# Forgetting attention with a SwiGLU block: q and k loaded by casting transfers, their factor moved behind the transpose

## The chip, the cores and the metric

The kernel runs on one core of one Trainium2 chip. A core has five engines with a queue of instructions each: PE (TensorE, matmuls and transposes; its weight loads are listed as PEld), DVE (VectorE), ACT (ScalarE), POOL (GpSimd) and SP (SyncE, which here only issues transfers). Besides these, 16 DMA engines move data between HBM and SBUF, 128 partitions wide; PE writes into PSUM, eight banks of 512 f32 values in each partition, and the other engines copy out of it. A transfer that SP or ACT issues goes through the hardware queues (q1 and q10 in the profile), one that POOL issues through the software queue (q0). In this kernel only the software queue's transfers change the type on the way, f32 in HBM to bfloat16 in SBUF.

The metric is the device time of one launch in microseconds (us). Of the kernel before there are three timed runs and one profiled execution.

## The reference

```python
# q, k, v: (8, 8, 576, 64) f32;  f: (8, 8, 576);  x: (4608, 512)
scores = np.matmul(q, k.transpose(0, 1, 3, 2)) / np.sqrt(64)      # factor 1/8
cum    = np.cumsum(np.log(np.clip(f, 0.0001, 1.0)), axis=-1)
decay  = cum[:, :, :, None] - cum[:, :, None, :]
scores = np.where(causal, -1e9, scores + decay)                   # row >= column
attn   = exp(scores - max) / (sum + 1e-9)
x      = np.matmul(attn, v).transpose(0, 2, 1, 3).reshape(4608, 512)
g, val = x @ w_gate, x @ w_val                                    # 512 -> 1536
out    = (g / (1 + np.exp(-g)) * val) @ w_out                     # 1536 -> 512
```

All matmuls of the kernel are in bfloat16 with f32 sums.

## The kernel before

**Tiling.** Two heads of a batch make a pair; there are 32 pairs p (four to a batch), each with 576 rows of q in nine blocks of 64. Block i of both heads lies on the 128 partitions at once (64 rows of either head), so a score tile is 128 by up to 512. A pair is worked in two groups, g = 0 with blocks 0 to 3 and g = 1 with blocks 4 to 8. For that, q is kept turned, 64 head values on partitions, with one head in the upper and one in the lower half of buffer `qz` and zeros in the other places; k is kept turned in `kt`.

**A pair's way.** SP loads k and q as f32 (line 453, buffers `kf` and `qf`); a row of a partition holds 6 consecutive rows of k (96 partitions) or 8 of q (72 partitions), for both heads. POOL copies them to bfloat16 (lines 481 and 483, buffers `qb` and `kb`), q times -1/8, and puts the two heads beside each other. PE transposes (line 207, `tx` in PSUM); ACT or DVE copies `tx` out to `kt` (one copy) or `qz` (two) at lines 509 and 511. PE forms the scores (line 201, `sp`); DVE adds the running sums of log f (`cb`), and for pairs from 16 on also a mask (`cm`), and takes the minimum of a row in the same instruction (line 652); ACT forms the exponential and its row sum (line 672, `e`); POOL scales each row by the reciprocal (line 708, `pk`). The probabilities are transposed into `pT`, for pairs 0 to 7 on PE with copies out (lines 737 to 743), for pairs from 8 on by a transfer that SP issues (line 721). PE multiplies with v (line 764), and the result is stored turned in `xT`, which holds a ring of 2048 tokens.

**The feed-forward part.** It goes over 12 tiles of tokens (256, 256, seven of 512, 256, 128, 128) as soon as their rows of `xT` are there: matmuls with `wg` and `wv` into `gv`, tanh on ACT (line 855), two products on DVE (lines 857 and 860), matmuls with `wo`, a copy out (lines 884 and 886), a transfer to HBM. The weights are loaded once, by POOL with a cast on the way (line 824 for `wg` and `wv`, in pieces of 256, 256, 512 and 512 columns each; line 828 for `wo`).

**The first four pairs** (`NHALF`) have a way of their own: their k and q come in parts (rows 0 to 255 and 256 to 575, of two neighbouring pairs together for k and for the first part of q), loaded at line 534, copied to bfloat16 at lines 560 to 564 on POOL, ACT or DVE, transposed, and copied out at lines 589 and 591. Their running sums are picked out by a matmul with ones (line 425) and copied to `cb` (line 430).

**The order.** All operations are first collected with a cost on each engine that may do them, the buffers that they read and write, and a priority. A planner (lines 63 to 195) then picks the operation that can start first by these costs, the smaller priority at a tie, gives it an engine and a buffer, and so writes out one order for each engine. `SLACK` says how long a buffer may be kept for a more urgent user. `STARTUP` is the order of the first transfers, written out by hand (k0: second part of k of pair 0; p4: k and q of pair 4; c: running sums; v01: part 1 of v of batch 0; wv2: the piece of `wv` that begins with column 256, and so on). A weight transfer on POOL also waits for the loads five places before it in that list and for the POOL load two before it. `NUDGE` shifts the priorities of single units (q4: all that prepares k and q of pair 4; a5.1: pair 5, group 1; f2: tile 2 of the feed-forward part; o: its second half; v: v of a batch). Loads of later pairs wait for the row sums of the pair four before.

```python
engs = {"POOL": 850 if p < 8 else 800 if name == "k" else 1010}
...
bufs("qb", [P, ROWS["q"][1], 2, D], BF16, 2)
bufs("kb", [P, ROWS["k"][1], 2, D], BF16, 2)
```

Of the kernel before, what the change touches and what calls it, by code (L numbers as in the profile page):

```python
# [8 lines left out]
F32 = mybir.dt.float32  # L9
# [198 lines left out]


def mm(*cols):  # L210
    return sum(max(29, c / 2.4 + 2.5) for c in cols)
# [3 lines left out]
def kernel(  # L215
# [45 lines left out]
    JFROM = 8  # L261
    TWO = False
    NDIRECT = 0

# [20 lines left out]
    NUDGE = "a0.0:-6 a1.0:-12.5 a10.0:1 a10.1:1.5 a12.0:-0.5 a13.0:0.5 a13.1:-1 a15.0:-1 a15.1:1 a16.0:-3 a17.0:-2 a17.1:-1.5 a18.0:-0.5 a21.0:-1 a21.1:-1 a22.1:0.5 a25.1:-1 a26.1:-1.5 a27.0:-1.5 a27.1:1 a29.0:2 a30.1:-1 a31.0:0.5 a31.1:0.5 a4.0:2.5 a4.1:2.5 a5.0:-1.5 a5.1:-1 a6.0:0.5 a6.1:1 a7.1:-0.5 a8.0:-1 a9.1:-0.5 f0:4 f1:2 f11:-4 f3:-5 f4:-3.5 f5:-4 f6:-2 f7:1 f8:9.5 f9:0.5 o0:-1 o1:-991 o10:-12.5 o11:3.5 o4:1 o5:-7 o6:-4.5 o8:1 o9:9 q0:-8.5 q1:-12 q10:-1.5 q11:-3 q12:-1.5 q13:-3 q14:-4 q15:-2 q16:-6 q17:1.5 q18:-4 q19:-2 q2:-10 q21:0.5 q24:0.5 q26:2.5 q27:0.5 q29:-2 q3:-9.5 q30:-4 q4:-7 q5:-5 q6:-1 q8:-1 v1:-5.5 v2:-2 v3:3.5 v4:1.5 v5:5.5 v6:0.5 v7:-5"  # L285

# [154 lines left out]
    def half(key):  # L441
        return pl.buf(key).bitcast(BF16)


    def load_pair(p):
        b, hp = divmod(p, NPB)
        s = first[p]
        if p < NHALF:
            load_parts(p)
            return  # L450
        for name, src, pr in (("k", k, 0), ("q", q, .1)):
            pl.key((name + "f", p), name + "f")
            loads[name, p] = pl.op({"SP": 620} if p else {"ACT": 620}, lambda e, name=name, src=src: (nc.scalar if e == "ACT" else nc.sync).dma_start(
                out=pl.buf((name + "f", p))[0:ROWS[name][0], :, :],
                in_=src[b, 2 * hp:2 * hp + 2].rearrange("h (p r) d -> p h (r d)", r=ROWS[name][1])),
                (), [(name + "f", p)], (-99 + 3 * p if p < NPB else s - SOON) + pr, dma=1060, pk=68 if name == "k" else 86, after=[sums[p - BACK, 0 if p - BACK >= NPB else 1]] if p >= NPB else [])
        if p >= NSEL:
            pl.key(("cb", p), "cb", p)
            for h in range(2):
                loads["cb", p, h] = pl.op({"SP": 600}, lambda e, h=h: nc.sync.dma_start(  # L460
                    out=pl.buf(("cb", p))[64 * h:64 * h + 64, :],
                    in_=cum_dram[2 * p + h:2 * p + h + 1, :].to_broadcast((64, S))),
                    ["cum_dram"], [("cb", p), (("cb", p), 3)], -98.5 + 3 * p if p < NPB else s - SOON + .2, dma=570, pk=93, after=[sums[p - CBACK, 0 if p - CBACK >= NPB else 1]] if p >= NPB + 1 else [])

    def prepare(p):
# [4 lines left out]
        for name in ("k", "q"):  # L470
            fk, bk = (name + "f", p), (name + "b", p)
            KR, KC = ROWS[name]
            pl.key(bk, name + "b")

            def cast(e, name=name, fk=fk, bk=bk, KR=KR):
                src = pl.buf(fk)[0:KR, :, :].rearrange("p h (r d) -> p r h d", d=D)
                dst = pl.buf(bk)[0:KR, :, :, :]
                if e == "ACT":
                    nc.scalar.activation(dst, src, AF.Copy, scale=-scale if name == "q" else 1.0)
                elif name == "q":  # L480
                    eng[e].tensor_scalar(dst, src, -scale, 1.0, op0=ALU.mult, op1=ALU.mult)  # L481
                else:
                    eng[e].tensor_copy(dst, src)
            engs = {"POOL": 850 if p < 8 else 800 if name == "k" else 1010}
            if p < NPB:
                engs = {"POOL": 850, "ACT": 850, "DVE": 500} if name == "k" else {"POOL": 1050, "ACT": 1050, "DVE": 680}
            o = pl.op(engs, cast, [fk], [bk], s - 1 + (name == "q") * .1)
            o.bias = SPARE if p else {}
            tk = ("tt", name, p)
# [4 lines left out]
            def transpose(e, bk=bk, tk=tk, KR=KR, KC=KC):  # L494
                src = pl.buf(bk).rearrange("p r h d -> p r (h d)")
                for j in range(KC):
                    turned(nc, half(tk)[:, KR * j:KR * j + KR], src[0:KR, j, :], ident[0:KR, 0:KR])
            pl.op({"PE": KC * (KR / 2.4 + 2.5)}, transpose, [bk], [tk, ok], s - 1, lat=200)
            halves = [(0, P, None)] if name == "k" else [(0, 64, 0), (64, 128, 1)]
            for a, z, h in halves:  # L500
                def evac(e, a=a, z=z, h=h, tk=tk, ok=ok, KC=KC):
                    if h is None:
                        src = half(tk)[a:z, 0:S].rearrange("r (j p) -> r p j", j=KC)
                        dst = pl.buf(ok)[a:z, :].rearrange("r (p j) -> r p j", j=KC)
                    else:
                        src = half(tk)[a:z, 0:S].rearrange("r (j i p) -> r i j p", j=R, i=NB)
                        dst = pl.buf(ok)[a:z, :, h, :].rearrange("r i (j p) -> r i j p", j=R)
                    if e == "ACT":
                        nc.scalar.copy(dst, src)  # L509
                    else:  # L510
                        nc.vector.tensor_copy(dst, src)
                o = pl.op({"ACT": 600, "DVE": 680 if h is None else 390}, evac, [tk] + ([("z", "qz", p)] if h is not None and p < len(pl.pools["qz"]) else []), [ok, (ok, "done")], s - .9)
                o.bias = LATER if p >= 8 else {}
# [9 lines left out]
    def load_parts(p):  # L523
        b, hp = divmod(p, NPB)
        pl.key(("cb", p), "cb", p)
        for name, x, a, z, r, n in parts(p):
            fk = (name + "f", p, x)
            pl.key(fk, name + "f")
            m = (z - a) // r

            def load(e, u, fk=fk, src=(k if name == "k" else q), a=a, z=z, r=r, m=m):
                h0 = 2 * (hp + u)
                (nc.scalar if e == "ACT" else nc.sync).dma_start(  # L533
                    out=pl.buf(fk)[m * u:m * u + m, :, 0:r * D],
                    in_=src[b, h0:h0 + 2, a:z].rearrange("h (p r) d -> p h (r d)", r=r))
# [12 lines left out]
    def prepare_parts(p):  # L548
        for name, x, a, z, r, n in parts(p):
            fk, bk, tk = (name + "f", p, x), (name + "b", p, x), ("tt", name, p, x)  # L550
            m = (z - a) // r
            pr = min(at[p + u, x == "B"] for u in range(n)) - 1 + (name == "q") * .1
            pl.key(bk, name + "b")
            pl.key(tk, "tx", line="q")

            def cast(e, name=name, fk=fk, bk=bk, r=r, w=m * n):
                src = pl.buf(fk)[0:w, :, 0:r * D].rearrange("p h (r d) -> p r h d", d=D)
                dst = pl.buf(bk)[0:w, 0:r, :, :]
                if e == "ACT":
# [13 lines left out]
            def transpose(e, bk=bk, tk=tk, r=r, w=m * n):  # L573
                src = pl.buf(bk).rearrange("p r h d -> p r (h d)")
                for j in range(r):
                    turned(nc, half(tk)[:, w * j:w * j + w], src[0:w, j, :], ident[0:w, 0:w])
            pl.op({"PE": r * (m * n / 2.4 + 2.5)}, transpose, [bk], [tk] + (oks if x == "A" else []), pr, lat=200, holds=oks)
# [239 lines left out]
    def weights():  # L817
        def piece(engs, fn, reads, writes, *a, **kw):
            loads[writes[0]] = pl.op(engs, fn, reads, writes, *a, **kw)

        cuts = [0, 256, 512, 1024, 1536]
        for a, z in zip(cuts, cuts[1:]):
            for nm, wt, src in (("wg", wg, moe_w_gate), ("wv", wv, moe_w_val)):
                piece({"POOL": 600}, lambda e, wt=wt, src=src, a=a, z=z: nc.gpsimd.dma_start(
                    out=wt[:, :, a:z], in_=src[:, a:z].rearrange("(ko p) n -> p ko n", p=P)),
                    (), [(nm, n) for n in range(a // P, z // P)], 2 + a / 256, dma=5.1 * (z - a) + 880, pk=20 if z - a == 256 else 42)
        for c in range(0, KF, 4):
# [120 lines left out]
    def unit(o):  # L948
        w = o.writes[0] if isinstance(o.writes[0], tuple) else (o.writes[0],)
        n, *i = w[0] + w[1:] if isinstance(w[0], tuple) else w  # L950
        if n in ("kb", "qb", "kt", "qz", "cm", "kf", "qf", "cb") or n == "tt" and isinstance(i[0], str):
            return f"q{i[0] if n != 'tt' else i[1]}"
# [52 lines left out]
```

## Time and profile before

| | before |
|---|---|
| median of 3 runs | 414.56 us (410.96, 414.56, 416.29) |
| profiled execution | 415.21 us |
| its span in the trace | 413.4 us, granted clock of TensorE 1.00 |
| PE busy | 392.5 us, 95% |
| DVE busy | 333.2 us, 81% |
| ACT busy | 320.5 us, 78% |
| POOL busy | 271.1 us, 66% |
| read from and written to HBM | 46.65 MB, 9.58 MB |
| bytes moved by all transfers | 72.16 MB, mean 175 GB/s |

An engine is busy while it executes; issuing a transfer, waiting and branching are not counted. The span goes from the first to the last instruction in the trace. A group of the profile reads: line, engine, operation, written buffer, read buffer, shapes, how many; then busy us in all, mean ns of one, and after the next bar the idle us of the engine just ahead of these instructions with what ended most of it. The chain of waits follows the end of the span back through what each step waited for.

### The profile page before, as it was taken

What the parts mean: (1) busy time and instruction counts of PE and PEld (TensorE: products, weight loads), DVE (VectorE), ACT (ScalarE), POOL (GpSimd) and SP (SyncE); (2) the same over time, 40 slices, a digit from 0 to 9 for tenths busy, and PEclk for the clock granted to TensorE, in tenths of its full rate; (3) what the DMA queues carried; (4) which work ended last, traced back from release to release, by engine and by line L of the source; (5) the groups of instructions that cost most, each with busy time, mean ns of one, the idle gap of its engine ahead of it and who ended that gap; (6) DMA issues with size and microseconds to landing.
All of it is one profiled execution on the core that took longest, in us unless ns stands there. A gap on an engine that the chain in (4) does not pass through costs nothing.

```text
span 413.4 us, 15350 instructions
## 1 busy us (share of the span) xinstructions
PE 392.5 (95%) x5848; PEld 269.3 (65%) x5848; DVE 333.2 (81%) x1270; ACT 320.5 (78%) x904; POOL 271.1 (66%) x475
## 2 busy tenths in 40 slices
PE   3988988889999999999999999999999999999996
PEld 2667878777666765567776666665566555568775
DVE  4799987798999789999998999899989952775232
ACT  5799988799999998979998897998899653332221
POOL 7679966699996887799789798878777340000000
PEclk9999999999999999999999999999999999999999
DMA  7999979879799999999999999978996744000211
GB/s 192 190 216 226 216 126 247 163 189 210 184 230 191 229 196 233 241 203 230 224 196 223 234 210 225 239 215 182 201 223 114 149 93 126 2 2 28 79 53 52
DMA packets 144026, 72.16 MB, mean 175 GB/s; under 512 B 117904, under 2 KB 131728, under 8 KB 143952
## 3 DMA queue, kind: packets, MB, share of 16 engines
q1 hardware_dynamic: 137856, 66.21, 74.4%
q0 software_dynamic: 5808, 4.72, 7.9%
q8 instruction: 45, 0.74, 0.8%
q14 instruction: 29, 0.24, 0.2%
q10 hardware_dynamic: 288, 0.26, 0.2%
HBM read 46.65 MB, written 9.58 MB: 136 GB/s over the span
## 4 chain that ended last, share of the span: by engine, by line
PE 81%; DMA 6%; DVE 5%; ACT 3%; issue 2%; POOL 1%; SPq 1%; POOLq 0%; ACTq 0%
PE gv L201 63%; PE sp L201 9%; PE tx L764 4%; PE tx L207 3%; DMA wg<-in_moe_w_gate_dram 3%; DVE t L652 3%; DMA kf<-in_k_dram 2%; PE gv L207 2%; DMA vf<-in_v_dram 1%; ACT eo L672 1%; ACT e L672 1%; SPq L533 1%; POOL vt L811 0%; DVE th L857 0%; ACT kt L509 0%
## 5 line engine op out<-in xcount | busy, mean ns | idle before, releaser
L652 DVE CUSTOM_DVE_ANT_0 t<-sp,cb 128x320 f32<-128x320 f32 (+7 forms) x272 | 121.7, 463 | 9.7 <-PE sp L201 5.1
L708 POOL TENSOR_SCALAR pk<-e,lr 128x512 bf16<-128x512 f32 (+3 forms) x189 | 101.5, 541 | 41.9 <-DVE lr L690 19.7
L201 PE MATMUL gv<-xT,wg 128*64 128x512 bf16 (+2 forms) x1152 | 112.7, 326 | 2.5 <-issue 1.4
L201 PE MATMUL gv<-xT,wv 128*64 128x512 bf16 (+2 forms) x1152 | 112.4, 326 | 0.1
L201 PE MATMUL gv<-wo,hh 128*64 128x512 bf16 (+1 forms) x888 | 106.5, 373 | 0.0
L857 DVE SCALAR_TENSOR_TENSOR th<-th,gv 128x512 f32<-128x512 f32 x108 | 73.9, 684 | 31.3 <-ACT th L855 30.5
L672 ACT ACTIVATE e<-t,tm 128x448 f32<-128x448 f32 (+4 forms) x160 | 88.9, 557 | 5.1 <-DVE tm L652 4.7
L855 ACT ACTIVATE th<-gv 128x512 f32<-128x512 f32 x108 | 64.3, 595 | 35.8 <-PE gv L201 35.2
L201 PE MATMUL sp<-kt,qz 128*64 128x512 bf16 (+7 forms) x640 | 77.9, 294 | 5.3 <-DVE tm L652 3.4
L708 POOL TENSOR_SCALAR pk<-eo,lr 128x256 bf16<-128x256 f32 (+3 forms) x128 | 70.4, 550 | 12.3 <-DVE lr L690 9.0
L201 PEld LDWEIGHTS <-wg 128*64 128x64 bf16 x1152 | 58.8, 110 | 30.0 <-issue 1.6
L201 PEld LDWEIGHTS <-wv 128*64 128x64 bf16 x1152 | 59.8, 110 | 27.4 <-issue 0.4
L860 DVE TENSOR_TENSOR hh<-th,gv 128x512 bf16<-128x512 f32 x108 | 73.7, 684 | 4.8 <-PE gv L201 1.8
L672 ACT ACTIVATE eo<-t,tm 128x256 f32<-128x256 f32 (+3 forms) x128 | 71.3, 558 | 4.3 <-DVE tm L652 3.1
L201 PEld LDWEIGHTS <-hh 128*64 128x64 bf16 x888 | 50.7, 110 | 31.3
L201 PEld LDWEIGHTS <-qz 128*64 128x64 bf16 x640 | 41.7, 113 | 23.0 <-issue 5.9
L884 ACT ACTIVATE ot<-gv 128x512 f32<-128x512 f32 (+1 forms) x34 | 19.9, 584 | 26.2 <-PE gv L201 26.0
L652 DVE DVE_READ_ACCUMULATOR2_ANT tm<- 128x1 f32 x432 | 35.7, 83 | 0.0
L652 DVE CUSTOM_DVE_ANT_0 t<-sp,cm,tm 128x64 f32<-128x64 f32 x128 | 34.4, 277 | 1.2 <-PE sp L201 0.3
L481 POOL TENSOR_SCALAR qb<-qf 72x1024 bf16<-72x1024 f32 x28 | 29.2, 1045 | 2.7 <-DMA qf<-in_q_dram 2.6
L672 ACT ACTIVATION_READ_ACCUMULATOR e<-t,tm 128x1 f32 x160 | 30.8, 193 | 0.0
L764 PE MATMUL tx<-pT,vt 128*64 128x320 bf16 (+4 forms) x448 | 29.6, 263 | 1.2 <-ACT pT L743 0.7
(73 smaller groups left out, 432.3 us busy)
## 6 DMA issues: line engine op xcount, KB each, us to landing
out_dram<-ot SPq DMA_DIRECT2D x35, 256.0 KB
vf<-in_v_dram SPq DMA_DIRECT2D x32, 256.0 KB
cb<-cum_f SPq DMA_DIRECT2D x56, 144.0 KB
kf<-in_k_dram SPq DMA_DIRECT2D x28, 288.0 KB
qf<-in_q_dram SPq DMA_DIRECT2D x28, 288.0 KB
wo<-in_moe_w_out_dram POOLq DMA_DIRECT2D x3, 512.0 KB, 7.0
vf<-in_v_dram SPq DMA_DIRECT2D x8, 128.0 KB
wv<-in_moe_w_val_dram POOLq DMA_DIRECT2D x2, 512.0 KB, 8.8
```

What stands on the lines that cost most here:

```text
L201: nc.tensor.matmul(out[c, :], lhsT[:, c], rhs, **kw)
L207: nc.tensor.transpose(out[c, :], src[:, c], ident)
L481: eng[e].tensor_scalar(dst, src, -scale, 1.0, op0=ALU.mult, op1=ALU.mult)
L533: (nc.scalar if e == "ACT" else nc.sync).dma_start(out=pl.buf(fk)[m * u:m * u + m, :, 0:r * D], in_=src[b, h0:h0 + 2, a:z].rearrange("h (p ...
L652: nc.vector.tensor_tensor_reduce(out=pl.buf(tk)[:, a:z], in0=pl.buf(sk)[:, o:o + z - a], in1=pl.buf(("cm", p))[:, i, :] if own else pl.buf ...
L672: nc.scalar.activation(pl.buf(ek)[:, :L], pl.buf(tk)[:, :L], AF.Exp, bias=pl.buf(("tm", p, g))[:, 0, i:i + 1], scale=-1.0, accum_out=pl.bu ...
L708: eng[e].tensor_scalar(dst, src, r, 1.0, op0=ALU.mult, op1=ALU.mult)
L764: nc.tensor.matmul(xo[r, 0:QB * n], vt[:, c, 2 * hp + h, :], pT[:, a:a + n, 64 * h:64 * h + 64], start=(c == 0), stop=(c == nch - 1))
L855: pl.op({"ACT": 487}, lambda e, u=u: nc.scalar.activation(pl.buf(("th", t, u)), pl.buf(("wg", t, u)), AF.Tanh, scale=0.5), [("wg", t, u)], ...
L857: pl.op({"DVE": 605}, lambda e, u=u: nc.vector.scalar_tensor_tensor(pl.buf(("th", t, u)), pl.buf(("th", t, u)), 1.0, pl.buf(("wg", t, u)), ...
L860: pl.op({"DVE": 605}, lambda e, u=u: nc.vector.tensor_mul(pl.buf(("hh", t, u)), pl.buf(("th", t, u)), pl.buf(("wv", t, u))), [("u", t, u), ...
L884: nc.scalar.mul(pl.buf(ok)[:, a:z], pl.buf(bk)[:, 0:z - a], 0.5)
```

## The change

1. **Loads.** For pairs 4 to 31, k and q are no longer loaded by SP as f32 and copied by POOL. POOL issues the transfer itself, straight from HBM into `kb` and `qb` in bfloat16 (56 transfers). The layout in these buffers is now head by head (a partition holds all its rows of one head, then of the other), so `turned_rows` transposes from a slice for each head instead of neighbouring columns. `kb` and `qb` get three buffers instead of two (`NQB`).
2. **Factor.** -1/8 is applied at the copy of `tx` to `qz`, on ACT by a multiply, on DVE by a tensor_scalar.
3. **Buffers of the first four pairs.** `qf` is gone: the f32 parts of q lie in the two buffers of `cm`, which hold masks only from pair 16 on. Their bfloat16 copies have buffers of their own (`kc`, `qc`), in the same head-by-head layout; their factor stays at line 562.
4. **Order.** `SLACK` goes from 400 to 250, `STARTUP` and `NUDGE` are new, and only POOL loads with a planned length above 1100 (the weights) still wait for the places before them in the list. Costs of other operations, tiles, groups and the places of the transposes of P stay.

```diff
+def turned_rows(nc, out, src, ident):
+    for h in range(2):
+        nc.tensor.transpose(out[64 * h:64 * h + 64, :], src[:, h, :], ident)
...
+    NQB = 3
+    CUTS = [0, 256, 512, 1024, 1536]
...
-    SLACK = 400
+    SLACK = 250
...
-    STARTUP = "p0 q1 f9 v01 k0 p2 wv2 q0 v04 wv0 wg2 wg0 k2 v00 c3 c1 q3 q2 wv4 v02 p4 c2 v03 c4 wg4 v11 c5 wv8 wg8 v10 v14 p5 v13 wo4 p6 v12 c6 wo0 c7 p7 wo8 c0"
+    STARTUP = "p0 f9 q1 k0 p2 v04 v01 wv2 q0 v00 wg0 wg2 k2 wv0 c1 c3 q3 wv4 v02 c0 p4 c2 q2 c4 wg4 v03 wg8 v11 c5 wv8 v10 p5 v12 v14 c6 v13 p6 wo0 p7 c7 wo4 wo8"
...
-    bufs("qf", [P, 2, ROWS["q"][1] * D], F32, 2)
-    bufs("kf", [P, 2, ROWS["k"][1] * D], F32, 2)
-    bufs("qb", [P, ROWS["q"][1], 2, D], BF16, 2)
-    bufs("kb", [P, ROWS["k"][1], 2, D], BF16, 2)
+    bufs("kf", [P, 2, 5 * D], F32, 2)
+    bufs("qc", [P, 2, 4 * D], BF16, 2)
+    bufs("kc", [P, 2, 5 * D], BF16, 2)
+    bufs("qb", [P, 2, ROWS["q"][1] * D], BF16, NQB)
+    bufs("kb", [P, 2, ROWS["k"][1] * D], BF16, NQB)
...
-            loads[name, p] = pl.op({"SP": 620} if p else {"ACT": 620}, lambda e, name=name, src=src: (nc.scalar if e == "ACT" else nc.sync).dma_start(
-                out=pl.buf((name + "f", p))[0:ROWS[name][0], :, :],
...
+            loads[name, p] = pl.op({"POOL": 560}, lambda e, src=src, bk=bk, w=ROWS[name]: nc.gpsimd.dma_start(
+                out=pl.buf(bk)[0:w[0], :, :], in_=src[b, 2 * hp:2 * hp + 2].rearrange("h (p r) d -> p h (r d)", r=w[1])),
+                (), [bk], (-99 + 3 * p if p < NPB else s - SOON) + pr, dma=1060, pk=42, after=[sums[p - BACK, 0 if p - BACK >= NPB else 1]] if p >= NPB else [])
...
-            o = pl.op(engs, cast, [fk], [bk], s - 1 + (name == "q") * .1)
...
-                    turned(nc, half(tk)[:, KR * j:KR * j + KR], src[0:KR, j, :], ident[0:KR, 0:KR])
+                    turned_rows(nc, half(tk)[:, KR * j:KR * j + KR], pl.buf(bk)[0:KR, :, D * j:D * j + D], ident[0:KR, 0:KR])
...
-                    if e == "ACT":
+                    if h is not None and e == "ACT":
+                        nc.scalar.mul(dst, src, -scale)
+                    elif h is not None:
+                        nc.vector.tensor_scalar(dst, src, -scale, None, op0=ALU.mult)
+                    elif e == "ACT":
                         nc.scalar.copy(dst, src)
...
-            pl.key(fk, name + "f")
+            pl.key(fk, "kf" if name == "k" else "cm")
...
-        if "POOL" in o.engs:
+        if "POOL" in o.engs and o.dma > 1100:
             o.after.append(line[n - BEHIND])
-            o.after += [x for x in line[:n] if "POOL" in x.engs][:-1][-1:]
+            o.after += [x for x in line[:n] if "POOL" in x.engs and x.dma > 1100][:-1][-1:]
```

More of the change, by code (lines that the diff above doesn't have):

```diff
@@ L442, in half, with rows @@
         return pl.buf(key).bitcast(BF16)
+    def rows(key):
+        x = pl.buf(key)
+        return x if key[0] == "kf" else x.rearrange("p i c -> p (i c)")[:, 0:8 * D].rearrange("p (h x) -> p h x", h=2)
     def load_pair(p):
@@ L451, in load_pair @@
         for name, src, pr in (("k", k, 0), ("q", q, .1)):
-            pl.key((name + "f", p), name + "f")
-            loads[name, p] = pl.op({"SP": 620} if p else {"ACT": 620}, lambda e, name=name, src=src: (nc.scalar if e == "ACT" else nc.sync).dma_start(
-                out=pl.buf((name + "f", p))[0:ROWS[name][0], :, :],
-                in_=src[b, 2 * hp:2 * hp + 2].rearrange("h (p r) d -> p h (r d)", r=ROWS[name][1])),
-                (), [(name + "f", p)], (-99 + 3 * p if p < NPB else s - SOON) + pr, dma=1060, pk=68 if name == "k" else 86, after=[sums[p - BACK, 0 if p - BACK >= NPB else 1]] if p >= NPB else [])
+            bk = (name + "b", p)
+            pl.key(bk, name + "b")
+            loads[name, p] = pl.op({"POOL": 560}, lambda e, src=src, bk=bk, w=ROWS[name]: nc.gpsimd.dma_start(
+                out=pl.buf(bk)[0:w[0], :, :], in_=src[b, 2 * hp:2 * hp + 2].rearrange("h (p r) d -> p h (r d)", r=w[1])),
+                (), [bk], (-99 + 3 * p if p < NPB else s - SOON) + pr, dma=1060, pk=42, after=[sums[p - BACK, 0 if p - BACK >= NPB else 1]] if p >= NPB else [])
         if p >= NSEL:
@@ L470, in prepare @@
         for name in ("k", "q"):
-            fk, bk = (name + "f", p), (name + "b", p)
+            bk = (name + "b", p)
             KR, KC = ROWS[name]
[L473 to L477, printed above, removed]
-                if e == "ACT":
[L479 to L486, printed above, removed]
-            o = pl.op(engs, cast, [fk], [bk], s - 1 + (name == "q") * .1)
-            o.bias = SPARE if p else {}
             tk = ("tt", name, p)
@@ L533, in load @@
                 (nc.scalar if e == "ACT" else nc.sync).dma_start(
-                    out=pl.buf(fk)[m * u:m * u + m, :, 0:r * D],
+                    out=rows(fk)[m * u:m * u + m, :, 0:r * D],
                     in_=src[b, h0:h0 + 2, a:z].rearrange("h (p r) d -> p h (r d)", r=r))
@@ L549, in prepare_parts @@
         for name, x, a, z, r, n in parts(p):
-            fk, bk, tk = (name + "f", p, x), (name + "b", p, x), ("tt", name, p, x)
+            fk, bk, tk = (name + "f", p, x), (name + "c", p, x), ("tt", name, p, x)
             m = (z - a) // r
             pr = min(at[p + u, x == "B"] for u in range(n)) - 1 + (name == "q") * .1
-            pl.key(bk, name + "b")
+            pl.key(bk, name + "c")
             pl.key(tk, "tx", line="q")
             def cast(e, name=name, fk=fk, bk=bk, r=r, w=m * n):
-                src = pl.buf(fk)[0:w, :, 0:r * D].rearrange("p h (r d) -> p r h d", d=D)
-                dst = pl.buf(bk)[0:w, 0:r, :, :]
+                src = rows(fk)[0:w, :, 0:r * D]
+                dst = pl.buf(bk)[0:w, :, 0:r * D]
                 if e == "ACT":
@@ L819, in piece @@
             loads[writes[0]] = pl.op(engs, fn, reads, writes, *a, **kw)
-        cuts = [0, 256, 512, 1024, 1536]
+        cuts = CUTS
         for a, z in zip(cuts, cuts[1:]):
@@ L825, in weights @@
                     out=wt[:, :, a:z], in_=src[:, a:z].rearrange("(ko p) n -> p ko n", p=P)),
-                    (), [(nm, n) for n in range(a // P, z // P)], 2 + a / 256, dma=5.1 * (z - a) + 880, pk=20 if z - a == 256 else 42)
+                    (), [(nm, n) for n in range(a // P, z // P)], 2 + a / 256, dma=5.1 * (z - a) + 880, pk={256: 20, 512: 42, 1024: 84}[z - a])
         for c in range(0, KF, 4):
@@ L950, in unit @@
         n, *i = w[0] + w[1:] if isinstance(w[0], tuple) else w
-        if n in ("kb", "qb", "kt", "qz", "cm", "kf", "qf", "cb") or n == "tt" and isinstance(i[0], str):
+        if n in ("kb", "qb", "kc", "qc", "kt", "qz", "cm", "kf", "qf", "cb") or n == "tt" and isinstance(i[0], str):
             return f"q{i[0] if n != 'tt' else i[1]}"
```

7 lines of the change are left out of this document (2 added, 5 removed).

## The prediction

> **What bounds the kernel now.** I read the page's busy times first, then the same busy times cut into stages, then the chain that ended last, then the waits of TensorE (PE) in the one stage in which it waits. First the page:
>
> ```profile
> span 413.4 us, 15350 instructions
> ## 1 busy us (share of the span) xinstructions
> PE 392.5 (95%) x5848; PEld 269.3 (65%) x5848; DVE 333.2 (81%) x1270; ACT 320.5 (78%) x904; POOL 271.1 (66%) x475
> ```
>
> PE is busy for 392.5 of 413.4 us, so no change that leaves PE's work alone can gain more than 20.9 us. The table of stretches says where these 20.9 us lie (columns: stretch, its length, then busy us and instructions of PE, PE's weight loads, DVE, ACT, POOL, then clock, DMA share, GB/s):
>
> ```profile
> 0.00:20.00 20.00, 12.17 (x120) 8.24 (x122) 12.15 (x48) 13.82 (x40) 13.67 (x46) 1.00 0.89 191
> 20.00:42.00 22.00, 18.87 (x358) 15.29 (x357) 20.60 (x79) 20.68 (x65) 19.51 (x35) 1.00 1.16 219
> 42.00:55.00 13.00, 11.21 (x265) 9.68 (x261) 11.93 (x38) 11.79 (x28) 8.82 (x15) 1.00 1.13 214
> 55.00:90.00 35.00, 30.85 (x676) 27.77 (x672) 28.16 (x96) 28.64 (x79) 26.96 (x45) 1.00 0.85 180
> 90.00:345.00 255.00, 254.27 (x3440) 163.50 (x3438) 226.87 (x963) 224.59 (x661) 202.12 (x336) 1.00 0.98 203
> ```
>
> From 90 to 345 us PE idles for 0.73 us in all, although DVE, ACT and POOL have work in that whole stretch: the feed-forward matmuls of tokens already attended to fill every hole. There an engine other than PE can become slower or faster by several us a pair without moving the end. What can move is the first 90 us: PE idles 7.83 us up to 20 us and 3.13 + 1.79 + 4.15 = 9.07 us from 20 to 90. In the stretch from 20 to 42 us DVE (20.60 of 22) and ACT (20.68 of 22) are both full. Two long pieces of the chain, in order of time (start, length, what), are transfers:
>
> ```profile
> 12.14 6.81 DMA kf<-in_k_dram
> 42.69 12.02 DMA wg<-in_moe_w_gate_dram
> ```
>
> The first is a k of the first pairs, whose path keeps its copy on POOL or another engine; the second is the last piece of the gate weights, issued by POOL at 42.69 and awaited by PE at 54.71. What PE itself loses there between 20 and 90 us (waiter, awaited, us in all, times, longest):
>
> ```profile
> PE sp L201 <- DVE tm L652: 3.2, 8, 1.0
> PE gv L201 <- issue: 1.4, 1, 1.4
> PE tx L207 <- issue: 1.4, 1, 1.4
> PE gv L201 <- DMA wg<-in_moe_w_gate_dram: 1.0, 2, 0.7
> PE tx L764 <- ACT pT L743: 0.7, 1, 0.7
> PE tx L207 <- POOL kb L564: 0.7, 1, 0.7
> ```
>
> So 3.2 us hang on DVE, 1.0 on weights, and the casts that the change removes (lines 481 and 483, buffers kb and qb) do not appear; the one POOL cast in the list, line 564, stays.
>
> **The change, part by part.** *Casts go, issues come.* POOL's groups, one shape each, the issues of the weights on POOL, and those of k and q on SP (min/median/max ns):
>
> ```profile
> L481 POOL TENSOR_SCALAR qb<-qf 72x1024 bf16<-72x1024 f32 x28 | 29.2, 1045 | 2.7 <-DMA qf<-in_q_dram 2.6
> L483 POOL CAST kb<-kf 96x768 bf16<-96x768 f32 x28 | 23.1, 825 | 0.9 <-DMA kf<-in_k_dram 0.8
> L824 POOL DMA_DIRECT2D wv<-in_moe_w_val_dram x4: 751/798/962, 9.9 to 40.2; - x4
> L453 SPq DMA_DIRECT2D qf<-in_q_dram x28: 306/404/1397, 28.2 to 305.8; - x28
> L453 SPq DMA_DIRECT2D kf<-in_k_dram x28: 313/470/2204, 25.2 to 305.4; - x28
> ```
>
> POOL loses 28 x (1.045 + 0.825) = 52.4 us and gets 56 issues. An issue of a casting transfer is on POOL in the trace only for the weights, at 0.80 us, with more rows a transfer than k and q have; the same k and q cost 0.40 and 0.47 us on SP. I take 0.80, the same engine and kind, and keep 0.44 as the other end: 56 x 0.80 = 44.8 us, or 24.6. Over the run POOL thus wins 7.6 us (up to 27.8), 22 or so pairs of it between 90 and 345 us, where PE waits for nothing: value 0. Up to 90 us the built order has POOL issue k and q of about six to seven pairs (12 to 14 issues, 9.6 to 11.2 us) where before it cast six pairs (6 x 1.87 = 11.2 us): 0 to 1.6 us, and POOL idles 2.49 + 4.18 + 8.04 = 14.7 us in these three stretches: value 0, at 0.44 us an issue a gain of up to 5 us on an engine that PE does not wait for.
>
> *What waits for the issues.* In the built order nearly every issue from pair 6 on waits for the transfer eight before it on POOL's queue, and from about pair 10 on most also for PE to have transposed pair p-3 out of the same of the three buffers. Behind a waiting issue stand POOL's normalizing copies (line 708), behind these SP's transposes of the probabilities, then PE's product with v. A pair of PE's work takes 255 us / 22 casts, some 11.6 us, and the buffer asked for is three pairs old; I price this wait at 0, and it is covered after 90 us in any case. SP loses 56 issues; v and the sums behind them start earlier, on a queue that no chain piece after 20 us names. Value 0.
>
> *The factor -1/8 and the transposes.* 56 copies of q out of PSUM get a multiply:
>
> ```profile
> L509 ACT COPY qz<-tx 64x576 bf16<-64x576 bf16 x40 | 25.3, 632 | 3.7 <-PE tx L207 1.7 <-DVE qz L511 1.5
> L884 ACT ACTIVATE ot<-gv 128x512 f32<-128x512 f32 (+1 forms) x34 | 19.9, 584 | 26.2 <-PE gv L201 26.0
> L511 DVE COPY qz<-tx 64x576 bf16<-64x576 bf16 x16 | 7.2, 453 | 3.1 <-PE tx L207 2.6 <-ACT qz L509 0.3
> L886 DVE TENSOR_SCALAR ot<-gv 128x512 f32<-128x512 f32 x3 | 2.1, 691 | 0.8 <-PE gv L201 0.8
> ```
>
> On ACT (42 of 56 in the new order) a scaled copy out of PSUM of 512 columns takes 584 ns on the average against 632 for the plain one of 576: no difference. On DVE (14) it lies between the plain 453 and the f32 one at 691 ns: at most 14 x 0.24 = 3.3 us, of which some six fall before 90 us (1.4 us); the nearest row is the copy of the same shape and type, so 0, with 1.4 kept for the range. PE's instructions are as many as before, with the same shapes. Value 0.
>
> *The order of the first pairs.* Counted up to the last score of the fourth pair, which DVE writes at 44 us, the built order takes from DVE four copies of k, one of cb, one of xT and one of pT, and three plain copies of q are replaced by smaller ones; it gives DVE one cast of q and one of v. ACT gets the four copies of k and the one of cb, and gives up two of its three first casts. The rows:
>
> ```profile
> L430 DVE COPY cb<-gv 128x256 f32<-128x256 f32 (+1 forms) x4 | 1.8, 441 | 2.0 <-PE gv L425 1.9
> L591 DVE COPY kt<-tx 128x256 bf16<-128x256 bf16 (+1 forms) x4 | 1.7, 455 | 0.8 <-PE tx L207 0.6
> L400 DVE TENSOR_SCALAR t<-t 64x576 f32<-64x576 f32 x1 | 0.5, 452 | 3.0 <-DMA t<-in_f_dram 3.0
> L589 ACT COPY kt<-tx 128x256 bf16<-128x256 bf16 (+1 forms) x4 | 1.4, 402 | 0.9 <-PE tx L207 0.9
> L560 ACT ACTIVATE kb<-kf 128x512 bf16<-128x512 f32 (+1 forms) x2 | 1.4, 675 | 0.9 <-DMA kf<-in_k_dram 0.9
> L430 ACT COPY cb<-gv 128x256 f32<-128x256 f32 x1 | 0.4, 372 | 1.0 <-PE gv L425 1.0
> ```
>
> DVE: 4 x 0.455 + 0.441 - 2 x 0.452 = 1.4 us less, and the other pieces, not priced here, are also fewer, so between 1 and 2.5 us less. ACT: 4 x 0.402 + 0.372 - 2 x 0.675 = 0.6 us more. Both are full from 20 to 42 us, and PE's waits name DVE: I take -1.5 us as DVE's gain, with +0.6 (ACT takes over) and -2.5 as ends.
>
> *Weights and k, q in one queue.* The new order puts k and q of pairs 4 and 5 between the last four weight pieces of POOL's queue. That queue (q0) from 10 to 29 us, when it carries pieces of 256 columns, and q1 and q0 from 29 to 56 us, with pieces of 512 (packets, MB, share of 16 engines), and how long the gate pieces took to land:
>
> ```profile
> q0 software_dynamic: 2112, 1.05, 45.6%
> ...
> q1 hardware_dynamic: 5285, 3.70, 61.1%
> q0 software_dynamic: 2112, 2.10, 49.5%
> ...
> DMA to landing us min/median/max: 8.0/9.3/12.0
> ```
>
> A packet of 512 columns costs 0.495 x 16 x 27 us / 2112 = 101 ns, one of 256 columns 0.456 x 16 x 19 / 2112 = 66 ns. A q of 72 x 2 rows of 512 values is 144 packets like the former, a k of 96 x 2 rows of 384 values 192 packets in between (84 ns). Two pairs: (288 x 101 + 384 x 84) / 16 = 3.8 us with all engines, 7.7 us at the 49.5% that q0 had. If q1, which sheds the same transfers, lends q0 its share, the last weight lands when it did. It is also no longer the gate piece: that one is issued ahead of about ten POOL operations that stood before it, and the value piece (wv) comes last, which PE wants some 3 us of matmuls later. I take 0, with +7.7 as one end and -1.0 (both weight waits gone) as the other.
>
> [...] The weights' issues took 751 to 962 ns while DVE was busy for nine tenths of 20 to 42 us. [...]
>
> **The sum.** 0 (casts, issues) + 0 (waits) + 0 (factor) - 1.5 (order of the first pairs) + 0 (weights) = -1.5 us. The profiled execution took 415.21 us, 1.8 us more than its span of 413.4, and the median of the three runs is 414.56. 415.2 - 1.5 gives 413.7, and from the median 413.1; I say **413.4 us**.
>
> **Rivals.** *A, the queue.* k and q of pairs 4 and 5 hold up the weights in q0. Place: PE's first value matmuls after 54 us. Price: 7.7 us later, 415.2 + 7.7 - 1.5 = **421.4 us**, slower than before. It decides when the last weight lands after about 58 us, 3 us past the 54.7 of now; up to there PE has other matmuls. For it: the queue serves in the order of issue, and landing already takes 8.0 to 12.0 us. Against: both queues together move the same bytes, and half the DMA engines' time is q1's.
> *B, the start closes up.* If freed POOL, DVE and an earlier gate piece remove all 9.07 us of PE's idle time from 20 to 90 us, 415.2 - 9.1 = **406.1 us**. For it: the fewer steps from transfer to transpose. Against: 2.8 of the 9.07 us are "issue" waits that nothing here touches, and ACT does not get lighter.
> [...]
> *D, nothing.* The start is bound by ACT as much as DVE, and the new order gains nothing: **415 us** (+0.6 at most).
>
> **How the numbers follow.** 2% of 414.56 is 8.3 us, about what a measurement of this kernel can tell from no change (its three runs lie between 410.96 and 416.29). Chances: forecast 0.45 (411 to 415), D 0.23, A 0.14, B 0.11, C 0.07. B taken whole ends at 406.1, just under 406.3, so most partial forms of it are within 2%: 0.07 for faster. A ends at 421.4, under 422.9, C at 423.4; with both partly at once, 0.10 for slower; 0.83 within 2%. The range leaves out the far halves of A, B and C, a little under two in ten: 407.5 to 420 us.
>
> **What would show it.** Right: POOL's busy time near 264 us (271.1 - 7.6), issues of kb and qb at 0.4 to 0.9 us, PE's idle time after 90 us under 1.5 us, its idle time from 20 to 90 us at 7 to 9 us, the q copies at 632 and 453 ns. [...] The forecast fails if PE's idle time from 0 to 20 us, which I leave as it is, changes: in the new order PE transposes a q of 80 rows and more k before its first score, which moves work ahead of the first DVE score, and I found no row to price that by.

## The result and the profile after

The changed kernel is slower: 437.51 us as the median of four runs (434.56 to 438.50) against 414.46 us, a ratio of 1.0555 with a 95% interval of 1.0469 to 1.0641. The prediction was 413.4 us, with 407.5 to 420. The profiled execution took 434.56 us. All ratios here leave disturbed runs out, so they can differ a little from the quotient of the medians beside them.

The page of the changed kernel:

```profile
span 432.6 us, 15279 instructions
PE 396.7 (92%) x5848; PEld 265.7 (61%) x5848; DVE 336.6 (78%) x1266; ACT 321.9 (74%) x908; POOL 259.6 (60%) x475
```

PE executes the same 5848 matmuls, but idles 432.6 - 396.7 = 35.9 us instead of 20.9: 15.0 us more. It is also busy 4.2 us longer. Together these are the 19.2 us by which the span grew. The stretches of the prediction again (length, busy us and instructions of PE, PEld, DVE, ACT, POOL, clock, DMA share, GB/s):

```profile
0.00:20.00 20.00, 11.14 (x108) 7.57 (x110) 10.24 (x34) 12.72 (x33) 13.03 (x45) 1.00 0.88 203
20.00:42.00 22.00, 17.96 (x328) 14.81 (x328) 20.24 (x83) 19.81 (x65) 19.72 (x36) 1.00 1.06 180
42.00:55.00 13.00, 12.20 (x298) 11.28 (x296) 12.41 (x47) 12.90 (x32) 10.32 (x18) 1.00 0.87 138
55.00:90.00 35.00, 34.60 (x760) 30.80 (x756) 33.02 (x117) 33.05 (x95) 29.24 (x52) 1.00 0.91 176
90.00:345.00 255.00, 236.44 (x3157) 143.68 (x3154) 216.57 (x903) 212.74 (x621) 181.94 (x317) 0.99 0.97 169
```

Up to 20 us PE idles 8.86 us instead of 7.83. From 20 to 90 us it idles 4.04 + 0.80 + 0.40 = 5.24 instead of 9.07. So the start, the only part that the prediction let move, gained 2.8 us. From 90 to 345 us PE idles 18.56 us where it had idled 0.73: there the loss lies. What PE waits for, from 90 to 320 us (waiter, awaited, us, times, longest):

```profile
PE tx L212 <- DMA qb<-in_q_dram: 10.3, 7, 4.2
PE tx L212 <- DMA kb<-in_k_dram: 5.7, 4, 1.8
PE sp L201 <- DVE tm L650: 2.5, 1, 2.5
```

16.0 of 18.5 us are the transposes, which stand in PE's queue until the new transfers have landed. The chain of waits shows it in one place (start, length, what):

```profile
99.12 6.58 DMA kb<-in_k_dram
...
105.74 0.45 PE tx L212 x12
...
108.55 8.62 DMA qb<-in_q_dram
...
117.21 0.47 PE tx L212 x16
...
121.94 9.37 DMA qb<-in_q_dram
```

Each transpose starts within 0.05 us of a landing. Feed-forward matmuls stand behind it in PE's queue and start only after it (behind the q that landed at 131.31 us: the transposes in the chain from 131.35 us, the feed-forward matmuls from 132.05 us). Most of the 4.2 us of longer busy time is the clock (the eighth column is the granted clock):

```profile
130.00:133.00 3.00, 1.65 (x22) 1.02 (x24) 1.10 (x5) 0.91 (x2) 3.00 (x6) 0.71 1.32 210
133.00:140.00 7.00, 7.00 (x92) 4.14 (x90) 4.21 (x18) 5.24 (x16) 1.58 (x5) 0.88 0.98 145
200.00:205.00 5.00, 2.62 (x34) 1.52 (x36) 0.24 (x1) 1.31 (x3) 3.02 (x5) 0.79 1.19 221
205.00:212.00 7.00, 7.00 (x96) 4.14 (x94) 6.28 (x30) 6.11 (x20) 4.27 (x8) 0.90 1.10 212
```

After two of the waits (2.1 us up to 131.3, 4.2 us up to 202.4) PE ran at half its clock for 3.4 us each. 3 x 0.29 + 7 x 0.12 + 5 x 0.21 + 7 x 0.10 = 3.5 us are lost by that. In the kernel before, the clock column reads 1.00 in every stretch up to 345 us. The three other runs of the changed kernel, 2.9 to 3.9 us longer, have a granted clock of 0.979 to 0.983 over the whole run, where this one has 0.991; so they lose more by it.

### The profile page after: what moved, and what is told of

The parts are those of the page before. It is cut to its first block, busy times and chain, and to the rows that moved or that the text cites. A ratio compares the mean times of both kernels' runs of the same rounds, so it can differ in the third digit from the quotient of the medians.

```text
span 432.6 us, 15279 instructions
## 1 busy us (share of the span) xinstructions
PE 396.7 (92%) x5848; PEld 265.7 (61%) x5848; DVE 336.6 (78%) x1266; ACT 321.9 (74%) x908; POOL 259.6 (60%) x475
## 4 chain that ended last, share of the span: by engine, by line
PE 53%; DMA 22%; POOL 12%; DVE 5%; issue 4%; ACT 3%; SPq 1%; POOLq 0%; DVEq 0%; ACTq 0%
PE gv L201 41%; DMA qb<-in_q_dram 14%; POOL pk L706 8%; DMA kb<-in_k_dram 6%; PE sp L201 5%; PE tx L212 3%; PE tx L762 3%; DVE t L650 2%; PE gv L207 1%; POOL vt L809 1%; DVE cm L605 1%; POOL kb L466 1%; DMA cm<-in_q_dram 1%; ACT e L670 1%; ACT eo L670 1%
## 5 line engine op out<-in xcount | busy, mean ns | idle before, releaser
L650 DVE CUSTOM_DVE_ANT_0 t<-sp,cb 128x256 f32<-128x256 f32 (+7 forms) x272 | 121.1, 464 | 24.6 <-PE sp L201 15.4
L706 POOL TENSOR_SCALAR pk<-e,lr 128x128 bf16<-128x128 f32 (+3 forms) x191 | 102.2, 538 | 46.0 <-DVE tm L650 12.0
L201 PE MATMUL gv<-xT,wv 128*64 128x512 bf16 (+2 forms) x1152 | 114.0, 329 | 0.0
L670 ACT ACTIVATE e<-t,tm 128x448 f32<-128x448 f32 (+4 forms) x160 | 88.7, 556 | 10.9 <-DVE tm L650 10.4
L201 PE MATMUL sp<-kt,qz 128*64 128x512 bf16 (+7 forms) x640 | 75.8, 297 | 6.9 <-DVE tm L650 6.8
L858 DVE TENSOR_TENSOR hh<-th,gv 128x512 bf16<-128x512 f32 x108 | 73.8, 684 | 10.4 <-PE gv L201 6.1
L706 POOL TENSOR_SCALAR pk<-eo,lr 128x384 bf16<-128x384 f32 (+2 forms) x127 | 68.4, 538 | 10.7 <-DVE lr L688 5.6
L201 PEld LDWEIGHTS <-hh 128*64 128x64 bf16 x888 | 49.1, 111 | 31.9 <-issue 1.1
L882 ACT ACTIVATE ot<-gv 128x512 f32<-128x512 f32 (+1 forms) x31 | 18.0, 580 | 25.4 <-PE gv L201 25.3
L504 ACT ACTIVATE qz<-tx 64x576 bf16<-64x576 bf16 x42 | 27.0, 642 | 9.7 <-PE tx L212 9.2
L605 POOL TENSOR_TENSOR cm<-cb,maskf 128x576 f32<-128x576 f32 x10 | 14.1, 1410 | 31.9 <-DVE tm L650 29.7
```

The lines of the kernel that those rows point to most:

```text
L201: nc.tensor.matmul(out[c, :], lhsT[:, c], rhs, **kw)
L504: nc.scalar.mul(dst, src, -scale)
L605: eng[e].tensor_tensor(pl.buf(("cm", p)), src, maskf.unsqueeze(1).to_broadcast((P, NB, QB)), op=ALU.add)
L650: nc.vector.tensor_tensor_reduce(out=pl.buf(tk)[:, a:z], in0=pl.buf(sk)[:, o:o + z - a], in1=pl.buf(("cm", p))[:, i, :] if own else pl.buf ...
L670: nc.scalar.activation(pl.buf(ek)[:, :L], pl.buf(tk)[:, :L], AF.Exp, bias=pl.buf(("tm", p, g))[:, 0, i:i + 1], scale=-1.0, accum_out=pl.bu ...
L706: eng[e].tensor_scalar(dst, src, r, 1.0, op0=ALU.mult, op1=ALU.mult)
```

## Experiments

**The theory.** The planner (line 172) reckons that a k or q on POOL's queue is there 2.85 + 1.06 + 0.5 = 4.4 us after its issue. How long the issues took on POOL in the changed kernel (ns, min/median/max):

```profile
L466 POOL DMA_DIRECT2D kb<-in_k_dram x28: 637/692/725, 30.7 to 301.0; - x28
L466 POOL DMA_DIRECT2D qb<-in_q_dram x28: 687/701/745, 31.4 to 301.6; - x28
```

How long it was from issue to landing, of qb and then of kb (the views of these two buffers):

```profile
DMA to landing us min/median/max: 3.8/7.3/12.1
```
```profile
DMA to landing us min/median/max: 3.0/5.7/10.7
```

The issue is short and regular, the landing is not. Two stretches of the same trace show what else the DMA engines do. First, 124.5 to 127 us, in which a q issued at 121.9 us is under way until 131.3; second, 239.5 to 241.5 us, with a k and a q that landed 3.6 and 5.1 us after their issue (queue, packets, MB, share of 16 engines):

```profile
q1 hardware_dynamic: 2063, 0.53, 117.8%
q0 software_dynamic: 50, 0.03, 7.3%
```
```profile
q0 software_dynamic: 395, 0.28, 93.4%
q1 hardware_dynamic: 12, 0.01, 1.7%
```

In the first, SP's queue moves 256-byte packets, the transposes of the probabilities that line 719 of the changed kernel issues, and the software queue gets 20 packets per us; in the second it has the engines to itself and gets 198. So the theory is L + T: the transfers land late because the transposes take the DMA engines (T), and the plan leaves less lead than that (L). Rivals: O, the newly planned order is what costs; Q, the issues come late because POOL's queue holds them; F, any plan that was not searched for costs as much. (Rival C in two of the texts below is T without L: the transfers come late however early they are asked for.)

**The old order in the changed kernel, and the new order in the kernel before.**

```diff
-    SLACK = 250
+    SLACK = 400
 ... and STARTUP, NUDGE: those of the kernel before (first run)
```

> The changed kernel with SLACK, STARTUP and NUDGE of the kernel before; loads, factor, buffers and transposes stay as changed, and the planner works out the order again. Theory L (k and q arrive too late): the planner reckons a k or q of POOL's queue to be there about 4.4 us after its issue (2.85 + 1.06 + 0.5), the changed kernel measured 6.5 (k) and 7.3 us (q) as medians and up to 12.1, and PE's transposes wait 16.0 us for them between 90 and 320 us. That is independent of the three constants, so PE waits for kb and qb again by more than 10 us and the time stays between 428 and 442 us. Theory O (the new order itself is what costs): the waits for kb and qb fall under 4 us and the time comes to between 412 and 419 us.

(The 6.5 us there is the median of k and q together; that of k alone is 5.7.)

> The kernel before with SLACK, STARTUP and NUDGE of the changed one; k and q are still loaded by SP as f32 and cast on POOL. Theory L: the constants were drawn for another set of operations, which costs a few us at most, PE idles less than 5 us between 90 and 320 us: 412 to 421 us. Theory O: PE idles more than 12 us there, 428 us or more.

Measured: 435.17 us, ratio to the kernel before 1.0455 (1.0405 to 1.0504), and 440.07 us, 1.0565 (1.0511 to 1.0619). PE's waits from 90 to 320 us, of the first run:

```profile
PE tx L212 <- DMA kb<-in_k_dram: 5.0, 2, 4.4
PE tx L212 <- DMA qb<-in_q_dram: 3.6, 1, 3.6
```

Of the second, and its row of that stretch:

```profile
PE sp L201 <- DVE tm L652: 11.5, 12, 4.6
```
```profile
90.00:320.00 230.00, 213.46 (x2871) 141.78 (x2867) 202.26 (x809) 189.34 (x547) 168.85 (x284) 0.96 0.93 199
```

The first falls to L rather than O: another order, and kb and qb are still the longest waits, though with 8.6 us not the "more than 10" that was expected. The second was expected wrongly. I had put the misfit of the constants at a few us; the kernel before loses 24 us with them, to waits for DVE (11.5 us) and to a clock of 0.96, and not to loads. In the changed kernel the new constants are no better than the old. So what the loads cost cannot be read from runs that plan anew. The next runs therefore keep the plan.

**The same plan, issues moved ahead.** The order that the planner wrote stays; only the issues of k and q are written earlier into POOL's queue, but behind the transposes that read the buffer before.

```diff
-        for o in pl.order():
+        LEAD = 4000
...
+        written = pl.order()
+        when = {o.n: (o.start, o.n) for o in written}
...
+                when[o.n] = min(when[o.n], max((o.start - LEAD, o.n), (clear.start, clear.n + .5)))
+        for o in sorted(written, key=lambda o: when[o.n]):
             o.fn(o.eng)
```

(`clear` stands for the transposes that last read the same buffer.)

> The changed kernel, with the same plan; only the issues of k and q of pairs 8 to 31 are written up to 4 us of planned time earlier into POOL's queue, though not ahead of the transposes that read the same buffer before. Theory L: a transfer that is asked for 4 us earlier is there 4 us earlier; the 11 waits of PE for kb and qb (16.0 us, the longest 4.2) go but for 2 us or so, and with them most of the halved clock (two stretches of 3.4 us at 0.5, some 3.4 us): 414 to 420 us. Rival C (the transfers are late because the DMA engines are shared with the transposes of the probabilities and running sums, however early they are asked for): flights grow to 10 us and more, the waits stay above 8 us, 426 us or more. Theory O: no change, 430 us or more.

> As the run with 4 us, with up to 8 us. Theory L: nothing left to gain beyond the 4 us run but the last waits; PE's waits for kb and qb under 1.5 us, 412 to 418 us. If POOL's queue instead stops at issues that wait for a buffer or for the transfer eight places before, its copies of the probabilities come later, PE waits at its product with v, and the time is above that of the 4 us run. Rival C: 426 us or more.

> As the run with 4 us, but the moved issues keep their order among themselves: there the k of one pair had been passed by the k and q of the next pair, whose issues wait for a buffer, and one wait of 3.3 us was left. Theory L: that wait goes, with the PE idle time behind it (3.3 of the 8.0 us between 90 and 320 us): 418 to 422 us. If keeping the order costs as much as it gives: 424 us.

> The same in order with up to 6 us. Theory L without a counterforce: 415 to 420 us, no wait of PE for kb or qb over 1 us. Theory B (an issue that comes too early stands in POOL's queue until PE has left the buffer, and holds up the copies of the probabilities behind it): PE's waits for pT at its product with v grow above 4 us and the time is 424 us or more, as the 8 us run had 6.7 us of them.

Medians: 424.31, 436.04, 425.73 and 432.18 us; ratios 1.0196 (1.0146 to 1.0246), 1.0493 (1.0430 to 1.0556), 1.0103 (1.0023 to 1.0182) and 1.0351 (1.0298 to 1.0403). The first, second and fourth median lie above what L gave; of the third, two of the four runs (420.02 and 423.63 us) come near its 418 to 422. These four had a fault of mine. Pairs are not loaded in the order of their numbers, and I took the lower number for the earlier user of a buffer. So single k and q were written over before PE had read them, some scores are formed from the k or q of another pair, and PE's transposes could wait for that later transfer. In the run with 8 us one wait was of this kind, the first of these:

```profile
PE tx L212 <- DMA kb<-in_k_dram: 8.4, 1, 8.4
PE tx L762 <- DMA pT<-pk: 6.7, 5, 2.7
```

It began at 104.7 us and ended at 113.0, with the landing of a k that was issued at 107.8 us. What these runs say of lead is therefore taken from the next three, which find the earlier user from the plan.

> Pairs are loaded in the order of their priorities (pair 13 ahead of 11 and 12), not by number; the four runs with moved issues took the lower number for the earlier user of a buffer, so that single k and q were written over those of another pair before PE had read them, and PE stood up to 8.4 us for that later transfer. Here the earlier user is taken from the plan; moved by up to 4 us. Theory L+T (the transfers land 2 to 5 us later than planned because the transposes of the probabilities share the DMA engines; more lead hides that): no wait of PE for kb or qb over 1 us, PE idle from 90 to 320 us at 4 to 9 us instead of 18.6, 418 to 424 us. Rival: the former gain came from the faulty buffers; 430 us or more.

> As with 4 us, moved by up to 6 us. L+T alone: as with 4 us or 1 to 3 us less, 415 to 423 us. Theory B (early issues stand in POOL's queue until PE has left the buffer, with the copies of the probabilities behind them): PE waits for pT at its product with v, 424 us or more.

> Moved by up to 8 us. L+T alone: 415 to 422 us. Theory B: 426 us or more, above the run with 4 us, with PE's waits for pT above 4 us.

Measured with 4, 6 and 8 us: 421.55, 422.79 and 426.75 us; ratios 1.0190 (1.0080 to 1.0299), 1.0174 (1.0086 to 1.0262) and 1.0269 (1.0194 to 1.0344). The waits of PE with 4 us, the stretch from 90 to 320 us with 4 us, and the longest wait with 8 us:

```profile
PE tx L762 <- DMA pT<-pk: 3.2, 2, 1.7
PE sp L201 <- DVE tm L650: 2.3, 3, 1.2
```
```profile
90.00:320.00 230.00, 224.32 (x3088) 158.47 (x3084) 204.80 (x871) 204.44 (x602) 176.51 (x307) 1.00 0.99 179
```
```profile
PE tx L762 <- DMA pT<-pk: 6.4, 3, 4.2
```

With 4 us no wait for kb or qb is left. PE idles 5.68 us there instead of 18.56, and the clock stays full. From issue to first transpose, over pairs 11 to 31, the trace has as medians 7.8 (k) and 9.4 us (q) in the changed kernel, PE's waits included, and 10.5 and 10.4 here; in the kernel before it was 9.0, with a cast on the way. 6 us and 4 us are the same within their intervals; with 6 us PE idles 4.54 us there and waits 1.8 us for pT, so no counterforce shows yet. With 8 us the time and the waits for pT are as theory B of these texts had them (it is not the prediction's rival B). But its mechanism, issues that stand in POOL's queue and hold up the copies of the probabilities, is not what this trace shows: POOL idles 1.1 us in all ahead of its issues of k and q. The transfer behind the longest wait was issued at 163.2 us, with 4 us of lead at 162.7, and landed after 14.9 us, where the median of its kind in this run is 7.6. Why it took so long, no run separates.

**The cause of the late landings.** Of each transfer that transposes probabilities, only the first of 25 blocks is left; the other 24 are not transposed.

```diff
-    out=both["pT"][pl.where[tk]], in_=both["pk"][pl.where[kk]].rearrange("p s k -> p (s k)")),
+    out=both["pT"][pl.where[tk]][:, 0:1, :], in_=both["pk"][pl.where[kk]].rearrange("p s k -> p (s k)")[:, 0:P]),
```

> The changed kernel in its own order; of each transfer that transposes the probabilities of pairs 8 to 31 only the first of 25 blocks is left, so 24 of 25 blocks are not transposed (and the output is not the reference's). Theory T (the flights of k and q are long because these transposes take the DMA engines): in the changed kernel the flights that overlap a transpose by under 1 us of all 16 engines' time take 4.6 us as the median, those with 2.5 us or more 7.0; so here all take 4 to 6 us, the median of q falls from 7.3 to 5.5 us or less, PE's waits for kb and qb from 16.0 us to under 7, and the time is 418 to 428 us. Rival Q (the issues come late because POOL's queue is held by other waits; the transposes do not matter): the flights may fall, but the waits stay above 11 us and the time above 430.

> The kernel before, with only the first of 25 blocks in each transfer that transposes the probabilities of pairs 8 to 31 (24 of 25 blocks are not transposed, and the output is not the reference's). It is the control for the same cut in the changed kernel, which took that one from 437 to 417 us. If the cut helps only where loads of k and q meet the transposes (theory T), the kernel before, whose PE idles 0.73 us from 90 to 320 us, gains under 3 us: 411 to 419 us. If the cut is worth as much anywhere: 400 us or less.

The changed kernel takes 417.16 us with it (one run; T had 418 to 428; the kernel before 417.06 as the median on the same chip). The kernel before takes 416.45 us against 416.62, a ratio of 1.0017 (0.9974 to 1.0059). So this shortening is worth nothing in the kernel before and some 20 us in the changed one (437.51 without it): T holds, and Q, which had 430 us or more, falls. PE's waits of transposes from 90 to 320 us in the changed kernel with short transfers, and the landings of qb and of kb:

```profile
PE tx L212 <- ACT e L670: 1.3, 1, 1.3
PE tx L212 <- DMA kb<-in_k_dram: 0.7, 1, 0.7
PE tx L212 <- DMA qb<-in_q_dram: 0.2, 1, 0.2
```
```profile
DMA to landing us min/median/max: 3.6/5.2/8.6
```
```profile
DMA to landing us min/median/max: 3.2/4.5/8.4
```

The profile puts the wait of 1.3 us down to ACT, but it ended at 172.97 us, 0.04 us after the landing of a q, so I count it with the loads. 16.0 us of waits became 2.2, with the same plan and the same issues in the same order; so F, that the plan alone costs this much, does not explain the loss. The short transfers also bring pT earlier, but the changed kernel had no wait for pT in this stretch. What changed is the landings: the medians fall from 7.3 to 5.2 and from 5.7 to 4.5 us, the longest from 12.1 to 8.6. Here the first transpose of pairs 11 to 31 comes 6.6 us after the issue (median). As PE hardly waits for loads here, I take that for the lead that the plan gives; a transfer that takes longer makes PE stand. PE still idles 5.0 us from 90 to 320 us in this run, 2.4 of them in one wait for DVE.

**Telling the planner.**

```diff
-                head, tail = (2850, 500) if q else ...
+                head, tail = (2850 if o.dma > 1100 else 5700, 500) if q else ...
```

> The changed kernel, with the planner told that a k or q of POOL's queue takes 2.85 us longer until it lands (5.70 instead of 2.85 us ahead of its packets); everything is planned anew with it. Theory L: the planner puts other matmuls of PE where the data are not yet there, or asks earlier; PE's waits for kb and qb fall from 16.0 to under 6 us, 418 to 428 us. Rival F (any plan that was not searched for is 20 us off, whatever the waits): 432 to 442 us, with waits of PE for DVE or ACT in their place.

436.16 us, ratio 1.0451 (1.0393 to 1.0509). PE's waits:

```profile
PE sp L201 <- DVE tm L650: 12.1, 14, 1.8
PE tx L212 <- DMA qb<-in_q_dram: 3.8, 1, 3.8
```

The waits for loads fell to 3.8 us as L has it, and the time did not fall: F. With a new plan 12.1 us of waits for DVE take their place, as in the second run above. That a new plan costs as much by itself does not take back the cause found in the old one.

## Why the prediction was wrong

- **The step that failed** stands in the first part and again under "What waits for the issues": "There an engine other than PE can become slower or faster by several us a pair without moving the end", and "it is covered after 90 us in any case". From 254.27 busy us out of 255 I concluded that there is cover. It only shows that in that order nothing came late. Feed-forward matmuls that stand behind a waiting transpose in PE's queue cover nothing. 16.0 us of waits for k and q, where there had been none, and 3.5 us of clock came out of this step; the other 2.5 of the 18.56 us are a wait for DVE.
- **The term that was missing** is the landing of k and q. I priced the issue (right: 0.69 and 0.70 us, within the 0.44 to 0.80 that I gave) and the wait for buffers. POOL hardly stood at its waits for lanes and buffers (the view of line 466 lists no idle time ahead of its issues either):

```profile
L466 POOLq EVENT_SEMAPHORE  x39: 17/17/43, 69.8 to 299.5; - x39
```

  But "flight against lead" was in no term, although the nearest rows were there: the gate pieces of the same queue, larger ones, had landed after 8.0 to 12.0 us. I used these rows for pairs 4 and 5 alone. With the figures measured since, a flight of 7.3 us (at most 12.1) against some 6.6 of lead, the price is up to 5.5 us for single ones of the 56 transfers.
- **Casts and issues:** POOL's busy time came to 259.6 instead of 264 us, as an issue took 0.70 and not 0.80; worth nothing in time, as said.
- **The factor:** 0 was right. The copies to qz with the factor, on ACT and DVE:

```profile
L504 ACT ACTIVATE qz<-tx 64x576 bf16<-64x576 bf16 x42 | 27.0, 642 | 9.7 <-PE tx L212 9.2
L506 DVE TENSOR_SCALAR qz<-tx 64x576 bf16<-64x576 bf16 x14 | 6.4, 455 | 1.1 <-PE tx L212 0.9
```

  642 against 632 ns, 455 against 453: under 0.5 us in all.
- **The order of the first pairs:** the gain was 2.8 us up to 90 us where I had 1.5, but not on DVE's side as argued. PE's waits for DVE from 20 to 90 us grew from 3.2 to 4.4 us; what went are the waits for weights (1.0), for copies of pT (1.2), for kb (0.7) and those called issue (2.8). That the size came near is luck:

```profile
PE sp L201 <- DVE tm L650: 4.4, 7, 1.2
PE gv L207 <- POOL pk L706: 0.5, 2, 0.3
```

- **The rivals.** A (k and q of pairs 4 and 5 hold up the weights) did not occur: PE waits for no weights at all. It named the right resource, the shared DMA engines, in the wrong place: not two pairs at the start but waits spread over 90 to 320 us, and with the transposes as what is in the way. C (at 423.4 us, with 0.69 us more for each issue on POOL) did not occur, and no run shows such an issue: the longest of the 56 took 745 ns, under the 0.80 us that I had priced. B came in part (3.8 of 9.07 us). D was not it.
- **What is left.** With 4 us of lead added, the changed kernel is still 1.9% slower (0.8 to 3.0), and none of the versions run beats the kernel before. In the profiled execution PE idles 5.68 us from 90 to 320 us instead of 0.73: 3.2 us for pT and 2.3 for DVE. That a searched order would win these back was not tried. Why the loads of the kernel before did not suffer is not settled either: they went through the same queue as the transposes, which no run separates from their lead of 9.0 us, and its trace has no landings of SP's transfers.

## What to carry to other kernels

That an engine is busy for 99.7% of a stretch does not say that a later input would be covered there, when its instructions start in the order in which they are written: ask of each of its inputs how long before use it is asked for, and how long it takes at worst. When a load changes its queue, compare flight with lead, and look for what else uses the DMA engines in that stage. A plan tuned to one set of operations is part of the kernel: with the other set's constants the kernel before was 24 us slower, more than the edit itself could give.

## What was not expected of the hardware

- **Sharing of the DMA engines.** Beside the 256-byte packets of the transposes, the software queue got 20 packets per us instead of 198. Between 90 and 320 us the flights of k and q had medians of 5.5 and 8.0 us, without 24 of 25 transposed blocks 4.1 and 4.9. By the packets as the profile counts them the two queues did not get even shares: 50 and 2063 in 2.5 us (124.5 to 127 us).
- **The clock.** Half clock followed a PE idle time of 2.1 us and one of 4.2 us: the clock column reads 0.50 from 131.27 to 134.68 us and from 202.95 to 206.36 us, 3.41 us each. Idle times of 1.7, 1.8, 2.0 and 2.5 us in the same trace had none. The two half-clock stretches began 71.68 us apart, which is 21.0 of their lengths. Divided from there into pieces of that length, the trace has these (length, then PE's busy us; the first two stand just before the half clock):

```profile
127.86:131.27 3.41, 1.38 (x28) 0.62 (x20) 3.24 (x11) 1.24 (x2) 2.65 (x5) 1.00 1.49 116
199.54:202.95 3.41, 0.57 (x20) 0.47 (x22) 0.44 (x3) 0.08 (x1) 1.61 (x2) 1.00 1.23 184
247.33:250.74 3.41, 1.58 (x26) 0.91 (x23) 2.87 (x15) 2.78 (x11) 1.71 (x2) 1.00 1.14 206
274.63:278.04 3.41, 2.11 (x20) 1.02 (x17) 3.41 (x3) 1.79 (x6) 3.41 (x7) 1.00 0.69 124
278.04:281.45 3.41, 2.25 (x27) 1.67 (x28) 3.37 (x15) 2.22 (x6) 3.35 (x7) 1.00 0.87 196
```

  The idle time of 2.5 us lies half in the fourth piece and half in the fifth. So in this trace, from 90 to 345 us, it is the idle share of such a piece, and not the length of one idle time, that goes with the half clock: it followed the two pieces with 0.57 and 1.38 us busy, and none of those with 1.58 us or more. Two cases give no limit. The late input of 2.1 us thus cost 3.8 us here: 2.1 us of waiting and 3 x 0.29 + 7 x 0.12 = 1.7 us by the clock.
